# One written order for all engines, and a softplus that stays in its PSUM bank

## The chip, the cores and the metric

The kernel runs on one core of a Trainium2 chip. The metric is the device time of one execution in microseconds (us), lower is better. TensorE (PE) does the matmuls, VectorE (DVE), ScalarE (ACT) and GpSimd (POOL) work on the tiles between them, SyncE (SP) starts the DMAs. Each engine runs its own instructions strictly in the order in which the program gives them, and waits on semaphores for what other engines produce.

## The reference

Three layers, each fed by the one before, all in float32:

```
attention   4 batches x 8 heads, x [512, 64] and state [32, 64] per head:
            x reads the state by softmax, the state reads x by softmax; 544 rows per batch
MoE 1       h = x @ w_in ;  g = softplus(h) ;  y = g @ w_out        d_model 512, d_ff 2048
MoE 2       silu(y @ w_gate) * (y @ w_val) @ w_out                  d_model 512, d_ff 1536
```

## The kernel before

**Numbers.** A float32 matrix product is made of three products of shorter floats (`mm3`, L90): each operand is split into a high part, written by ScalarE, and a low part, whole minus high, written by `low` (L93). So every operand of a product costs a ScalarE pass and a VectorE or GpSimd pass, and each product is a high·high, a low·high and a high·low matmul.

**Stages.** The first 60 us or so are the attention. Then come the 64 units of MoE 1, numbered n = 0 to 63: d_ff is cut into four chunks c of 512, a chunk goes over the four batches b, and each of these over four pieces ft of 128 columns. A unit's first product `p1` (named pn here, 6 matmuls, L90 `ph`) puts h into one PSUM bank. ScalarE takes the softplus of it twice, once rounded into the high part `h` and once whole into a tile `C` in SBUF (class `Softplus`, L477 and L480). GpSimd makes the low part (`g_low`, gln here). The second product (Pn, `py`, 12 matmuls) runs several units later. From about 350 us on stand the 24 steps of MoE 2, named q, a, b, c, th and tL in the written order, with w_gate, w_val and w_out split piece by piece ahead of them.

**Seven products.** For three pairs of batches (chunk 1 batches 2 and 3, called pair 1 here; chunk 2 batches 2 and 3, pair 2; chunk 3 batches 0 and 1, pair 3) the second product is done as a 2 x 2 block product with seven instead of eight products. The blocks of g are B11 and B21 (first batch, ft 0-1 and 2-3) and B12 and B22 (second batch). `g_sum` (L598, VectorE) forms T1 = B12 − B11, T3 = B22 − B12, T2 = T3 + B11 and T4 = B21 − T2 for each of two halves f; T3 overwrites B12's SBUF tile. Each sum is split (`g_split_high` on ScalarE, L604; `g_split_low` on GpSimd). The products run in the order P1, P2, P5, P3, P6, P7, P4 (`y_part`, `pyPP`), 12 matmuls each, in units 24 to 30, 40 to 46 and 48 to 54. Each has two halves i in two banks. P6, P7 and P4 go on accumulating in P1's banks, P3 in those of P5. After each product `y_part_add` adds both halves to the running sum `yacc` (`y_put`, L533, VectorE; yan and ybn here for i = 0 and 1). P3 may write into P5's banks only after VectorE has read P5 out of them: P27 waits for ya26 and yb26, P43 for ya42 and yb42, P51 for ya50 and yb50.

**Weights.** Beside this the weights of the next chunk are loaded and split by `Piece`: ab ("size", ScalarE), hd ("head", L144, VectorE), tl ("tail", L155 and L158, two VectorE passes), wh (ScalarE) and wl (GpSimd). The piece's name follows: w is w_in, o is w_out of MoE 1, e are the pieces of MoE 2. In the traces they are `t_win`, `t_wo` and `t_gv`. `m_pair` folds w_in into the state's matmul (`pm`): mm on PE, mh on ScalarE, ml on VectorE (`m`, L93).

**PSUM.** There are eight banks of 128 x 512 floats. Tiles are requested by a tag ("y", "h" or "m"), and one that finds no free bank waits until an older one has been read.

**What sets the order.** Two passes with a manual schedule. The head (up to unit 8) is a written list, `ORDER`. From unit 9 on, a loop over n runs hooks (`at(n, kind, ...)`) of the kinds load, pe, dve0, act, pool, dve2, dve1, act1, pool1, so an operation's place is a rule, the same in each pair. MoE 2 has steps of its own (`at2`).

Of the kernel before, what the change touches and what calls it, by code (L numbers as in the profile page):

```python
# [18 lines left out]
LOADS = "x00 x01 st x21 x20 w0 x11 x10 x31 x30 w3 w2 n20 n21 w1 n01 n11 n10 n00 n31 o1 o0 o3 n30 o2"  # L19
ORDER = (  # L20
# [11 lines left out]
)  # L32

FIRST = 9


@with_exitstack
def attention_moe_moe2_kernel(
# [77 lines left out]
    class Piece:  # L116
# [52 lines left out]
        def low(self):  # L169
            low(nc.gpsimd, self.out[:, 1, :], self.t, self.out[:, 0, :])  # L170
# [14 lines left out]
    class GatePiece(Piece):  # L185
# [11 lines left out]
        def low(self):  # L197
            super().low()
# [16 lines left out]
        def split_sums(self):
            o = slot([P, 2, 512], F32R, self.place(), f"split_{self.name}")
            nc.scalar.activation(o[:, 0, :], self.s, AF.Copy)  # L217
            low(nc.gpsimd, o[:, 1, :], self.s, o[:, 0, :])
# [4 lines left out]
    class OutPiece(Piece):  # L223
# [8 lines left out]
        def low(self):  # L232
            super().low()
# [4 lines left out]
        def sums(self):  # L238
            pass

        def split_sums(self):
            pass
# [3 lines left out]
    def second_piece(f, part, late=False):  # L246
# [17 lines left out]
    class OutSums:  # L264
# [10 lines left out]
        def whole(self):  # L275
            self.t = []
            for f, r in enumerate(self.raw):
                t = rawp.tile([P, 512], F32, tag="tmade", bufs=3, name=f"w2t{self.q}_{f}")
                nc.vector.tensor_tensor(out=t, in0=r[:, 0].bitcast(F32), in1=r[:, 1].bitcast(F32), op=ALU.add)
                self.t.append(t)  # L280

        def sums(self):
            (a11, a21), (a12, a22) = ((t[:, :256], t[:, 256:]) for t in self.t)
            self.s = [rawp.tile([P, 512], F32, tag="sums", bufs=2, name=f"w2u{self.q}_{k}") for k in range(2)]
            s = [self.s[k // 2][:, k % 2 * 256:(k % 2 + 1) * 256] for k in range(4)]
            for o, x, y, op in (
# [3 lines left out]
                nc.gpsimd.tensor_tensor(out=o, in0=x, in1=y, op=op)  # L290

        def high(self):
            self.o = [slot([P, 2, 512], F32R, "made", f"w2o{self.q}_{k}") for k in range(2)]
            for k, o in enumerate(self.o):
                nc.scalar.activation(o[:, 0, :], self.s[k], AF.Copy)

        def low(self):
            w2s_d[self.q] = dram.tile([P, 2, 2, 512], F32, tag=f"w2s{self.q}", name=f"w2s{self.q}_d")
            for k, o in enumerate(self.o):
                low(nc.gpsimd, o[:, 1, :], self.s[k], o[:, 0, :])  # L300
                nc.sync.dma_start(out=w2s_d[self.q][:, k], in_=o.bitcast(F32))
# [15 lines left out]
    room = ["y"]  # L317

    class Item:
# [50 lines left out]
        def minus(self):  # L370
            m1 = self.mine("m1", 16)
            nc.gpsimd.tensor_tensor(
# [14 lines left out]
        def times(self):  # L387
            r1 = self.mine("r1", 16)
            nc.gpsimd.tensor_tensor(
# [11 lines left out]
        def low(self):  # L401
            low(nc.gpsimd, self.out[:, 1, :], self.t2, self.out[:, 0, :])

        def turn_e(self):
            self.ps = bank(room[0], f"pa{self.n}")
# [7 lines left out]
        def read(self):  # L413
            b, par = self.b, self.par
            self.ps = bank(room[0], f"pr{self.n}")
# [14 lines left out]
    def st_turn(b):  # L430
        srp[b] = bank(room[0], f"psr{b}")
# [24 lines left out]
    def m_pair(c, b):  # L456
        for par, tag in enumerate("mh"):
            m_mm(c, b, par, tag)

    def m_pair_high(c, b):  # L460
        for par in range(NPAR):
            m_high(c, b, par)

    def m_pair_low(c, b):
        for par in range(NPAR):
            m_low(c, b, par)


    class Softplus:


        def __init__(self, ps, g, h):
            self.ps, self.g, self.h = ps, g, h
# [5 lines left out]
        def whole(self):  # L479
            nc.scalar.activation(self.g, self.ps, AF.Softplus)  # L480
# [4 lines left out]
    def p1(u):  # L485
# [15 lines left out]
    def g_low(u):  # L501
        if sp[u].h is None:
            return
        l = work.tile([P, 512], F32R, tag="GL", bufs=BIG, name="l%d_%d_%d" % u)
        low(nc.gpsimd, l, sp[u].g, sp[u].h)
# [6 lines left out]
    def p2(u):  # L512
        c, b, ft = u
        if ft == 0:
            for dt in range(KT):
                yps[dt] = bank("y", f"py{c}_{b}_{dt}")
        t = gT.pop(u)
        for dt in range(KT):
            mm3(yps[dt], [wo[c, ft].out[:, i, dt * P:(dt + 1) * P] for i in range(2)], t, ft == 0, ft == FT - 1)

    def y_add(c, b, dt):
        y_put(b, dt, yps[dt], c == 0)
# [11 lines left out]

    SEVEN = {(1, 1), (2, 1), (3, 0)}
# [13 lines left out]
    class WoSums:  # L549
# [5 lines left out]
        def sums(self):  # L555
# [6 lines left out]
            for o, x, y, op in (  # L562
# [3 lines left out]
                nc.vector.tensor_tensor(out=o, in0=x, in1=y, op=op)  # L566

        def high(self):
            for k in range(2):
                o = ws[self.c, k, self.i] = slot([P, 2, 512], F32R, "ws", f"ws{self.c}_{k}_{self.i}")  # L570
                nc.scalar.activation(o[:, 0, :], self.s[k], AF.Copy)

        def low(self):
            for k in range(2):
                o = ws[self.c, k, self.i]
                low(nc.gpsimd, o[:, 1, :], self.s[k], o[:, 0, :])
# [11 lines left out]
    def g_sum(c, q, t, f):  # L588
# [4 lines left out]
        a, b = (g_whole(c, q, k, f) for k in (x, y))  # L593
        if at is None:
# [3 lines left out]
        nc.vector.tensor_tensor(out=o, in0=a, in1=b, op=op)  # L598
# [12 lines left out]
    def y_part(c, q, part):  # L611
        kind, k, t = OUTS[part]
        keep = KEEP[part]
        for i in range(2):
            if part in OPENS:
                ypx[keep, i] = bank("y", f"pyP{part}_{c}_{q}_{i}")
            ps = ypx[keep, i]
# [91 lines left out]
    def s4(c):  # L709
        if c == 0:  # L710
            ys[0] = const.tile([P, DM], F32, tag="yo", bufs=2, name="ys")
            nc.vector.tensor_copy(ys[0], tps["s3"])
        else:
            nc.vector.tensor_tensor(out=ys[0], in0=tps["s3"], in1=ys[0], op=ALU.add)

    def turn_ys():
        yT[0] = const.tile([P, 2, KT, P], F32R, tag="sy", name="yT")
        v = turn_mm(ys[0], KT, "ys")
        nc.scalar.activation(yT[0][:, 0], v, AF.Copy)
        low(nc.vector, yT[0][:, 1], v, yT[0][:, 0])  # L720
# [9 lines left out]
    banks = [0]  # L730

    def quad_bank(name):
        banks[0] += 1
        return bank("h" if banks[0] % 4 else "m", name)
# [13 lines left out]
    def split_act(key, src):  # L748
        h = work.tile([P, 512], F32R, tag="AH", bufs=7, name="h%d_%s" % key)
        l = work.tile([P, 512], F32R, tag="AL", bufs=7, name="l%d_%s" % key)  # L750
        nc.scalar.activation(h, src, AF.Copy)  # L751
        low(nc.gpsimd, l, src, h)
        act[key] = (h, l)

# [14 lines left out]

    def out_mm(n, j, dt):  # L770

        q = n % NF // 2
        b = 2 * (n // NF) + j
        ps = bank("y", f"po{n}_{j}_{dt}")
        for f in range(2):
            mm3(ps, [w2[n + f][:, i, dt * P:(dt + 1) * P] for i in range(2)], act[n + f, j], f == 0, f == 1)
        out_add(b, dt, ps, q == 0)
        if q == NQ - 1:
            out_store(b, dt)


# [3 lines left out]
    def out_part(n, part):  # L785
# [498 lines left out]
```

## Time and profile before

| | |
|---|---|
| median of 3 runs | 742.68 us (742.31 to 744.7) |
| the profiled execution | 743.8 us, its span 742.0 us |
| mean granted clock of TensorE over the span | 0.983 |
| DMA | 134.88 MB, mean 182 GB/s |

The span is the time from the first to the last instruction of the profiled execution; 1.8 us lie around it. Page section 2 cuts the span into 40 slices and gives the busy tenths of every engine in each; PE stands at 9 in nearly all, with exceptions that the tables by stretch show better. A busy PE there can also be one at half the clock: the granted clock stands beside it.

### The profile page before, as it was taken

How to read it: one execution, taken by the hardware profiler on the slowest of the kernel's cores; microseconds unless marked ns; L12 is line 12 of the kernel's file. 1: busy time of each engine (PE TensorE's matmuls, PEld its weight loads, DVE VectorE, ACT ScalarE, POOL GpSimd, SP SyncE). 2: the span in 40 equal slices, each digit the busy share in tenths (PEclk: the TensorE clock that was granted, in tenths of full speed). 3: DMA queues.
4: the chain of work that ended last, by engine and by line, in shares of the span. 5: the costliest groups of instructions: out<-in, count | busy, mean ns of one | idle time of the engine just before them, and what ended most of it. 6: DMA issues, size and time to landing. Idle time of an engine off the chain costs nothing.

```text
span 742.0 us, 10249 instructions
## 1 busy us (share of the span) xinstructions
PE 710.4 (96%) x3654; PEld 567.1 (76%) x3654; DVE 548.0 (74%) x768; ACT 345.5 (47%) x641; POOL 456.1 (61%) x355
## 2 busy tenths in 40 slices
PE   5699999999899979899999999999999999999997
PEld 1477877786678767688888888888888888888885
DVE  5875553789679897958489988889785666665564
ACT  3876464635454436443355544454453334343231
POOL 2467634698668786864157776577786367464252
PEclk9899999999899999999999999999999999999999
DMA  9910202253124330081463886767559997969303
GB/s 341 408 61 28 86 29 57 59 198 114 57 86 159 126 114 1 0 315 62 157 213 99 276 292 247 250 246 282 199 210 361 353 333 283 374 216 343 122 1 114
DMA packets 48627, 134.88 MB, mean 182 GB/s; under 512 B 5441, under 2 KB 17729, under 8 KB 48577
## 3 DMA queue, kind: packets, MB, share of 16 engines
q1 hardware_dynamic: 48576, 134.24, 50.9%
q8 instruction: 28, 0.46, 0.2%
q14 instruction: 23, 0.18, 0.1%
HBM read 93.06 MB, written 41.16 MB: 181 GB/s over the span
## 4 chain that ended last, share of the span: by engine, by line
PE 76%; DVE 15%; ACT 3%; issue 2%; POOL 2%; DMA 1%; SPq 0%; DVEq 0%; ACTq 0%
PE px L90 16%; PE py L90 16%; PE po L90 8%; PE ph L90 8%; PE pz L90 8%; PE poP L90 6%; PE pyPP L90 5%; PE pt L90 3%; DVE C L598 2%; PE ps L687 2%; DVE yacc L533 2%; PE pm L446 1%; PE ps L90 1%; DVE m L93 1%; DVE t_wo L155 1%
## 5 line engine op out<-in xcount | busy, mean ns | idle before, releaser
L93 POOL TENSOR_TENSOR l<-C,h 128x512 fp32r<-128x512 f32 x58 | 83.8, 1449 | 48.1 <-ACT C L480 42.7
L90 PE MATMUL ph<-aT,m 128*128 128x512 f32 x384 | 100.1, 399 | 0.2 <-DVE m L93 0.2
L90 PE MATMUL py<-h,wo 128*128 128x512 f32 x320 | 99.4, 391 | 0.9 <-POOL wo L93 0.8
L90 PEld LDWEIGHTS ph<-aT,m 128*128 128x128 f32 x384 | 71.3, 190 | 24.9 <-issue 7.5
L90 PEld LDWEIGHTS py<-h,wo 128*128 128x128 f32 x320 | 60.0, 188 | 14.5 <-POOL wo L93 1.6
L90 PE MATMUL po<-h,w 128*128 128x512 f32 x224 | 69.6, 392 | 0.0
L90 PE MATMUL py<-l,wo 128*128 128x512 f32 x160 | 62.3, 390 | 0.0
L93 POOL TENSOR_TENSOR split_gv<-sums_gv,split_gv 128x512 fp32r<-128x512 f32 x24 | 35.4, 1473 | 31.7 <-ACT split_gv L217 26.1
L477 ACT ACTIVATE h<-ph 128x512 fp32r<-128x512 f32 x58 | 34.4, 592 | 42.4 <-PE ph L90 42.3
L765 DVE TENSOR_TENSOR oacc<-poP,oacc 128x512 f32<-128x512 f32 x62 | 40.7, 687 | 10.3 <-PE poP L90 10.3
L90 PEld LDWEIGHTS po<-h,w 128*128 128x128 f32 x224 | 41.6, 188 | 8.5
L1139 POOL TENSOR_TENSOR cC<-cC,cB 128x512 f32<-128x512 f32 x24 | 32.0, 1332 | 21.0 <-ACT cB L1138 15.1
L90 PE MATMUL po<-l,w 128*128 128x512 f32 x112 | 43.7, 390 | 0.0
L480 ACT ACTIVATE C<-ph 128x512 f32<-128x512 f32 x64 | 38.0, 594 | 9.0 <-PE ph L90 9.0
L765 DVE TENSOR_TENSOR oacc<-po,oacc 128x512 f32<-128x512 f32 x48 | 31.9, 684 | 13.9 <-PE po L90 13.7
L93 POOL TENSOR_TENSOR l<-cA,h 128x512 fp32r<-128x512 f32 x14 | 19.9, 1418 | 32.8 <-ACT h L751 31.2
L90 PE MATMUL px<-T_0s,gw 128*128 128x512 f32 x135 | 38.1, 390 | 0.7 <-ACT cA L1177 0.7
L1203 DVE TENSOR_TENSOR cA<-py,cA 128x512 f32<-128x512 f32 x22 | 15.1, 685 | 31.8 <-PE py L90 26.6
L90 PE MATMUL px<-T_1s,gw 128*128 128x512 f32 x135 | 38.0, 389 | 0.0
L93 POOL TENSOR_TENSOR gv<-t_gv,gv 128x512 fp32r<-128x512 f32 x24 | 34.3, 1430 | 5.4 <-ACT gv L167 5.4
L533 DVE TENSOR_TENSOR yacc<-pyPP,yacc 128x512 f32<-128x512 f32 x42 | 28.4, 683 | 8.9 <-PE pyPP L90 8.9
L90 PEld LDWEIGHTS py<-l,wo 128*128 128x128 f32 x160 | 30.0, 188 | 6.3
(263 smaller groups left out, 1870.2 us busy)
## 6 DMA issues: line engine op xcount, KB each, us to landing
gw<-gv_d SPq DMA_DIRECT2D x60, 512.0 KB, 7.8
gv_d<-gv SPq DMA_DIRECT2D x24, 512.0 KB, 6.5
gv_d<-split_gv SPq DMA_DIRECT2D x24, 512.0 KB, 4.9
raw_win<-in_moe_w_in_dram SPq DMA_DIRECT2D x16, 512.0 KB, 6.5
raw_wo<-in_moe_w_out_dram SPq DMA_DIRECT2D x16, 512.0 KB, 3.6
w<-w_d SPq DMA_DIRECT2D x13, 512.0 KB, 9.4
raw_gv<-in_moe_w_gate_dram SPq DMA_DIRECT2D x48, 128.0 KB, 3.6
raw_gv<-in_moe_w_val_dram SPq DMA_DIRECT2D x48, 128.0 KB, 3.5
```

The source lines that it names most:

```text
L90: nc.tensor.matmul(o, a[s], b[t], start=first and i == 0, stop=last and i == 2, **k)
L93: eng.tensor_tensor(out=o, in0=whole, in1=high.bitcast(F32), op=ALU.subtract)
L155: nc.vector.scalar_tensor_tensor(out=ti, in0=self.top, scalar=-0x80000000, in1=ti, op0=ALU.bitwise_and, op1=ALU.bitwise_or,)
L446: nc.tensor.matmul(ps[k * NS:(k + 1) * NS, :], st[q, k, b, :], win[c, k].t[q, :], start=True, stop=True)
L477: nc.scalar.activation(self.h, self.ps, AF.Softplus)
L480: nc.scalar.activation(self.g, self.ps, AF.Softplus)
L533: nc.vector.tensor_tensor(out=v, in0=ps, in1=v, op=ALU.add)
L598: nc.vector.tensor_tensor(out=o, in0=a, in1=b, op=op)
L687: nc.tensor.matmul(gs[c][:, f], win[c, kt].t[:, f], sw[:, kt, :], start=kt == 0, stop=kt == KT - 1)
L765: nc.vector.tensor_tensor(out=v, in0=ps, in1=v, op=ALU.add)
L1139: nc.gpsimd.tensor_tensor(out=c["C"], in0=c["C"], in1=c["B"], op=ALU.mult)
L1203: nc.vector.tensor_tensor(out=c["A"], in0=y, in1=c["A"], op=ALU.add)
```

## The change

One table `ORDER` now names every operation of the whole program, 2121 names, and a loop runs it from front to end; the hooks, `at`, `at2` and the loops over n are gone. Functions that did several things are cut into one per operation, so that each has a name; many get their engine as an argument ("!" behind a name means the other one of VectorE and GpSimd). The operations themselves are the same, with the same engines, but for the softplus below. On SP, x11's load goes behind x31's, and one weight load (lw21) ahead of another piece's; on PE one group of six matmuls (s3m.4) moves some 10 us ahead.

The order changes on VectorE, ScalarE and GpSimd in a few dozen places, the most of them in the head and in the three pairs. For the first pair, VectorE's order before and after (/0 and /1 are the two passes of a tail):

```
before  hd.e1.0 tl.w22 tl.e1.0 ya23 yb23 yc23 yd23 g.T1110 hd.o20 ml.200 ml.201 g.T1111 ya24
        g.T3110 yb24 hd.o22 g.T2110 ya25 g.T3111 yb25 tl.o22 ml.210 ml.211 g.T2111 ya26 g.T4110
        yb26 tl.o20 g.T4111 ya27
after   hd.e1.0 tl.w22 tl.e1.0 ya23 yb23 yc23 yd23 g.T1110 hd.o20 ml.200 ml.201 g.T1111 ya24
        gl30 g.T3110 yb24 hd.o22 g.T2110 gl31 g.T3111 tl.o22 yb25 ml.210 ml.211 ya26 ya25 g.T4110
        yb26 g.T2111 tl.o20 g.T4111 ya27
```

For the second pair:

```
before  hd.w33 tl.w33 hd.e2.1 tl.w32 tl.e2.1 ya39 yb39 yc39 yd39 g.T1210 hd.o30 ml.300 ml.301
        g.T1211 ya40 g.T3210 yb40 hd.o32 g.T2210 ya41 g.T3211 yb41 tl.o32 ml.310 ml.311 g.T2211
        ya42 g.T4210 yb42 tl.o30 g.T4211 ya43
after   tl.w32 hd.w33 tl.w33 hd.e2.1 tl.e2.1 ya39 yb39 yc39 yd39 g.T1210 hd.o30 ml.300 ml.301
        g.T1211 ya40 gl46 g.T3210 hd.o32 yb40 g.T3211 g.T2210 ya41 gl47 yb41 ml.310 ya42 tl.o32
        g.T2211 g.T4210 yb42 tl.o30 ml.311 g.T4211 ya43
```

In the third pair gl54 and gl55 are put in behind ya48 and ya49; else the order around ya50 stays. On ScalarE, ab.e1.0 goes ahead of sh.e0.1. In the head, tl.o03 goes ahead of S5, S4 and r4 on VectorE, and wl.o03 ahead of ti5 on GpSimd. In MoE 2, a3.1 goes ahead of tl.e3.1.

The softplus of the second batch of each pair:

```diff
     class Softplus:
-        def __init__(self, ps, g, h):
+        def __init__(self, ps, g, h, stay=False):
...
         def whole(self):
-            nc.scalar.activation(self.g, self.ps, AF.Softplus)
+            if self.stay:
+                nc.scalar.activation(self.ps, self.ps, AF.Softplus)
+            if self.g is not None:
+                nc.scalar.activation(self.g, self.ps, AF.Copy if self.stay else AF.Softplus)
...
-        g = work.tile([P, 512], F32, tag="G", bufs=BIG, name=f"C{n}")
-        if (c, b // 2) in SEVEN and b % 2 and ft < 2:
-            sp[u] = Softplus(ps, g, None)
+        seven = (c, b // 2) in SEVEN and b % 2
+        g = None if seven and ft >= 2 else work.tile([P, 512], F32, tag="G", bufs=BIG, name=f"C{n}")
+        h = None if seven and ft < 2 else work.tile([P, 512], F32R, tag="GH", bufs=BIG, name=f"h{n}")
+        sp[u] = Softplus(ps, g, h, seven)
...
+    def g_low(u, eng):
         l = work.tile([P, 512], F32R, tag="GL", bufs=BIG, name="l%d_%d_%d" % u)
+        if sp[u].g is None:
+            low(nc.vector, l, sp[u].ps, sp[u].h)
         else:
-            sp[u] = Softplus(ps, g, work.tile([P, 512], F32R, tag="GH", bufs=BIG, name=f"h{n}"))
...
+            low(eng, l, sp[u].g, sp[u].h)
...
-    def g_sum(c, q, t, f):
+    def g_sum(c, q, t, f, eng):
...
         a, b = (g_whole(c, q, k, f) for k in (x, y))
+        if x in ("B12", "B22"):
+            a = sp[c, 2 * q + 1, BLOCK[x][1] + f].ps
```

So of the second batch, units ft 0 and 1 (block B12: units 28, 29, 44, 45, 52 and 53) get their softplus in place in the bank, and then a ScalarE copy of it to SBUF. Units ft 2 and 3 (B22: 30, 31, 46, 47, 54, 55) get the high part into SBUF and the softplus in place; they have no whole tile in SBUF any more. T1 and T3 read B12 and B22 from the bank, and the low part of the six B22 units is made by VectorE from the bank instead of by GpSimd from SBUF. A bank is then held until VectorE has read it for T1, or for T3 and the low part.

## Rows read from the trace of the kernel before

**Rows 1.** Stretches: PE, PEld, DVE, ACT, POOL busy us (instructions), granted clock, DMA share, GB/s.

```profile
180.00:200.00 20.00, 15.81 (x73) 12.89 (x72) 15.66 (x18) 6.99 (x14) 13.88 (x9) 0.83 0.25 79
260.00:280.00 20.00, 15.79 (x79) 12.97 (x78) 18.40 (x23) 7.97 (x16) 15.31 (x10) 0.91 0.32 105
300.00:320.00 20.00, 17.58 (x70) 13.68 (x69) 17.86 (x22) 10.21 (x20) 17.36 (x13) 0.91 0.13 37
```

**Rows 2.** Waits of PE: what for, us in total, times, longest.

```profile
PE pyPP L90 <- DVE yacc L533: 10.7, 3, 4.2
```

**Rows 3.** Timeline of PE at its gaps: start, us, instructions, [idle before <- releaser].

```profile
60.52 0.50 PE L90 MATMUL py<-h,wo 128*128 128x512 f32 x1 [0.84 <-POOL wo L93]
...
188.42 1.22 PE L90 MATMUL pyPP<-h,ws 128*128 128x512 f32 x2 [4.19 <-DVE yacc L533]
...
269.85 1.22 PE L90 MATMUL pyPP<-h,ws 128*128 128x512 f32 x2 [4.21 <-DVE yacc L533]
...
310.29 1.16 PE L90 MATMUL pyPP<-h,ws 128*128 128x512 f32 x2 [2.27 <-DVE yacc L533]
...
382.94 0.97 PE L90 MATMUL px<-T_0s,gw 128*128 128x512 f32 x3 [0.68 <-ACT cA L1177]
```

**Rows 4.** The chain that ended last, pieces in order of time: start, us, what.

```profile
57.03 1.44 DVE t_wo L158
...
188.42 5.49 PE pyPP L90 x12
...
199.14 2.74 PE pyPP L90 x12
...
269.85 4.41 PE pyPP L90 x12
...
310.29 4.62 PE pyPP L90 x12
```

**Rows 5.** Timeline of DVE before the first gap.

```profile
162.63 1.07 DVE L144 TENSOR_SCALAR t_gv<-t_gv 128x512 int32<-128x512 int32 x1 [2.40 <-ACT t_gv L135]
...
169.44 2.48 DVE L533 TENSOR_TENSOR yacc<-py,yacc 128x512 f32<-128x512 f32 x4
...
181.99 1.18 DVE L155 SCALAR_TENSOR_TENSOR t_wo<-raw_wo,t_wo 128x512 int32<-128x512 int32 x1
183.21 1.66 DVE L158 SCALAR_TENSOR_TENSOR t_wo<-raw_wo,t_wo 128x512 int32<-128x512 int32 x1
...
185.99 1.78 DVE L598 TENSOR_TENSOR C<-C,C 128x512 f32<-128x512 f32 x1
187.69 0.68 DVE L533 TENSOR_TENSOR yacc<-pyPP,yacc 128x512 f32<-128x512 f32 x1
```

**Rows 6.** Groups of instructions: busy us, mean ns of one | idle before.

```profile
L533 DVE TENSOR_TENSOR yacc<-pyPP,yacc 128x512 f32<-128x512 f32 x42 | 28.4, 683 | 8.9 <-PE pyPP L90 8.9
L598 DVE TENSOR_TENSOR C<-C,C 128x512 f32<-128x512 f32 x18 | 22.8, 1269 | 0.0
L93 POOL TENSOR_TENSOR l<-C,h 128x512 fp32r<-128x512 f32 x58 | 83.8, 1449 | 48.1 <-ACT C L480 42.7 <-PE pyPP L90 5.3
```

**Rows 7.** Timeline of ACT before the first pair.

```profile
161.42 0.63 ACT L217 ACTIVATE split_gv<-sums_gv 128x512 fp32r<-128x512 f32 x1 [2.23 <-POOL sums_gv L213]
161.96 0.64 ACT L135 ACTIVATE t_gv<-raw_gv 128x512 f32<-128x512 f32 x1
```

**Rows 8.** Timeline of DVE before the second and the third gap.

```profile
243.50 1.01 DVE L144 TENSOR_SCALAR t_gv<-t_gv 128x512 int32<-128x512 int32 x1 [2.48 <-ACT t_gv L135]
...
269.11 0.68 DVE L533 TENSOR_TENSOR yacc<-pyPP,yacc 128x512 f32<-128x512 f32 x1
...
309.56 0.68 DVE L533 TENSOR_TENSOR yacc<-pyPP,yacc 128x512 f32<-128x512 f32 x1
```

**Rows 9.** Timeline of PE: the first product of unit 30.

```profile
168.85 1.65 PE L90 MATMUL ph<-aT,m 128*128 128x512 f32 x6
```

**Rows 10.** Timeline of DVE in MoE 2: the first pass of tl.e3.1.

```profile
378.46 1.59 DVE L151 SCALAR_TENSOR_TENSOR t_gv<-t_gv,raw_gv 128x512 int32<-128x512 int32 x1
```

More of the change, by code (lines that the diff above doesn't have):

```diff
@@ L236, in low, with second_piece @@
             nc.sync.dma_start(out=w2_d[self.f], in_=self.out.bitcast(F32))
[L238 to L242, printed above, removed]
     made = {}
-    def second_piece(f, part, late=False):
+    EARLY = {(f, part) for f in range(3) for part in range(2)} | {(0, 2)}
+    def second_piece(f, part):
+        late = (f, part) not in EARLY
         return OutPiece(f, late) if part == 2 else GatePiece(f, part, late)
@@ L289, in sums, with high, low @@
             ):
[L290 to L301, printed above, removed]
+                eng.tensor_tensor(out=o, in0=x, in1=y, op=op)
+            self.o = {}
+        def high(self, k):
+            self.o[k] = slot([P, 2, 512], F32R, "made", f"w2o{self.q}_{k}")
+            nc.scalar.activation(self.o[k][:, 0, :], self.s[k], AF.Copy)
+        def low(self, k, eng):
+            if self.q not in w2s_d:
+                w2s_d[self.q] = dram.tile([P, 2, 2, 512], F32, tag=f"w2s{self.q}", name=f"w2s{self.q}_d")
+            o = self.o[k]
+            low(eng, o[:, 1, :], self.s[k], o[:, 0, :])
+            nc.sync.dma_start(out=w2s_d[self.q][:, k], in_=o.bitcast(F32))
     def load_w2s(q):
@@ L316, in attention_moe_moe2_kernel @@
     small = {}
-    room = ["y"]
     class Item:
@@ L456, in m_pair @@
     def m_pair(c, b):
-        for par, tag in enumerate("mh"):
+        for par, tag in enumerate("my" if c == 0 and b < 2 else "mh"):
             m_mm(c, b, par, tag)
[L460 to L466, printed above, removed]
     class Softplus:
-        def __init__(self, ps, g, h):
-            self.ps, self.g, self.h = ps, g, h
+        def __init__(self, ps, g, h, stay=False):
+            self.ps, self.g, self.h, self.stay = ps, g, h, stay
         def high(self):
@@ L729, in attention_moe_moe2_kernel, with quad_bank @@
     }
[L730 to L734, printed above, removed]
+    def quad_bank(n, k):
+        return bank("m" if (3 * n + k) % 4 == 3 else "h", f"p{'xzy'[k]}{n}")
     def quad_mm(ps, n, part, first):
@@ new lines, in attention_moe_moe2_kernel, with op, either @@
+        ops = {}
+        def op(name, fn, *args):
+            ops[name] = lambda: fn(*args)
+        def either(name, fn, *args, eng=nc.gpsimd):
+            other = nc.vector if eng is nc.gpsimd else nc.gpsimd
+            ops[name] = lambda: fn(*args, eng)
+            ops[name + "!"] = lambda: fn(*args, other)
+        for k in range(B * NPAR):
+            it = Item(*divmod(k, NPAR))
+            for key, step in (
+                ("sc", it.scores), ("mx", it.most), ("nm", it.negate), ("e", it.exp_tokens), ("rc", it.parts),
+                ("ts", it.turn_scores), ("M", it.maxima), ("ex", it.exps), ("S", it.sums),
+                ("r", it.parts_1), ("tu", it.turn), ("ah", it.high),
+                ("pa", it.turn_e), ("a", it.turned), ("pr", it.read), ("sr", it.mean),
+            ):
+                op(f"{key}{k}", step)
+            for key, step in (("mi", it.minus), ("ti", it.times), ("al", it.low)):
+                either(f"{key}{k}", step)
@@ L1010, in attention_moe_moe2_kernel @@
-        at(NU - 4, "pe", turn_ys)
-        for n in range(2):
-            at(NU - 5 + n, "load", load_gw, n)
-        at(NU - 3, "load", load_w2, 0)
+            op(f"ld.{name}", begin)
+            for tag, step in (("ab", "size"), ("hd", "head"), ("tl", "tail"), ("wh", "high"), ("sh", "split_high")):
+                op(f"{tag}.{name}", lambda step=step: getattr(store[key], step)())
+            for tag, step in (("wl", "low"), ("sm", "sums"), ("sl", "split_low")):
+                either(f"{tag}.{name}", lambda eng, step=step: getattr(store[key], step)(eng))
@@ new lines, in attention_moe_moe2_kernel, with softplus @@
+        for f in range(NF):
+            for part in range(3):
+                piece_ops(f"e{f}.{part}", made, (f, part), second_piece)
+        def softplus(u):
+            sp[u].high()
+            sp[u].whole()
+        for n, u in enumerate(units):
+            op(f"p{n}", p1, u)
+            op(f"sp{n}", softplus, u)
+            either(f"gl{n}", g_low, u, eng=nc.gpsimd)
+            c, q, k = u[0], u[1] // 2, n % (2 * FT)
+            if (c, q) in SEVEN:
+                part = SEQUENCE[k]
+                op(f"P{n}", y_part, c, q, part)
+                for i in range(2):
+                    op(f"y{'ab'[i]}{n}", y_part_add, c, q, part, i)
+            else:
+                op(f"P{n}", p2, u)
+                for dt in range(KT):
+                    op(f"y{'abcd'[dt]}{n}", y_add, c, u[1], dt)
@@ new lines, in attention_moe_moe2_kernel, with fresh, total, quad @@
+        op("tys", turn_ys)
+        op("tysh", turn_ys_high)
+        op("tysl", turn_ys_low)
+        NS2 = NPR * NF
+        cs = {n: {} for n in range(NS2)}
+        def fresh(n, k):
+            cs[n][k] = work.tile([P, 512], F32, tag=k, name=f"c{k}{n}")
+            return cs[n][k]
+        def total(eng, o, x, y, op):
+            eng.tensor_tensor(out=o(), in0=x(), in1=y(), op=op)
+        def quad(n, part):
+            if part in ("P1", "P5", "P2"):
+                k = ("P1", "P5", "P2").index(part)
+                cs[n]["xzy"[k]] = quad_bank(n, k)
+            quad_mm(cs[n][QUAD_KEEP[part]], n, part, part in ("P1", "P5", "P2"))
@@ L1246 @@
+                for name in names.split():
+                    ops[name]()
 _INS = ['moe_w_in', 'moe_w_out', 'moe2_w_gate', 'moe2_w_val', 'moe2_w_out']
```

635 lines of the change are left out of this document (203 added, 432 removed), and 141 rows, old and new, of tables (ORDER, STEPS).

## The prediction

> **What bounds the kernel now.** First the page: PE is busy 96% of the span, no other engine over 74%. So PE sets the time, and only PE's gaps, and the stretches in which it runs slowly, can be won back. The stretches show where these lie: three of 20 us have a granted clock below 1 and PE busy below 20 us [rows 1], and each holds one of the three pairs. The waits name the cause: three waits of a `pyPP` product for VectorE's `yacc`, 10.7 us in all [rows 2]. PE's timeline places them: P27 at 188.42 after 4.19 us, P43 at 269.85 after 4.21, P51 at 310.29 after 2.27 [rows 3]. The chain shows a second price. The twelve matmuls behind the wait take 5.49, 4.41 and 4.62 us, where the same twelve take 2.74 us at 199.14 [rows 4]: after the idle time the clock is at the lower of its two levels (1.2 against 2.4 GHz) for some of them, 0.83 on the mean of the first stretch [rows 1]. That is 2.75 + 1.67 + 1.88 = 6.3 us on top, 17.0 us together. Beside these there are a gap of 0.84 us in the head, for GpSimd's `wo`, and one of 0.68 us in MoE 2, for ScalarE's cA [rows 3]. All five are 18.5 us. That is the most that a better order could bring while the work stays, and PE's own work stays: the same matmuls in the same order but for one group.
>
> **Pair 1.** VectorE decides when P27 starts, so its queue is summed. Before, it idles 2.40 us ahead of hd.e1.0, for ScalarE's ab.e1.0 [rows 5]. This op stands on ScalarE behind sh.e0.1, which waits for GpSimd's sums while ScalarE idles 2.23 us [rows 7]. Moved ahead, ab.e1.0 fills that idle time, and hd.e1.0 starts at 160.2 instead of 162.63. Nothing else stands between it and ya23 in either order, so ya23 comes at 169.44 − 2.4 = 167.0 (what it reads, P23's first quarter, has been made by then). From ya23 to ya26 it is 187.69 − 169.44 = 18.25 us before [rows 5]. Of this:
> - ya25 (0.6 us from start to start, as the four adds in 2.48) and g.T2111 (1.7 to the next start) go behind ya26: −2.3.
> - gl30 and gl31 are new on VectorE: six such in all, two per pair, and no row shows this op. The nearest is `yacc`, one operand in PSUM and one in SBUF, 683 ns [rows 6], 0.6 us from start to start: +1.2. From above it is bounded by the slow two-SBUF-input op of 1.27 us, +2.5; below 0.6 nothing of this shape runs.
> - T3110 and T3111 read one operand from PSUM now. With both in SBUF an op of L598 takes 1269 ns on the mean, 1.78 at worst, beside a busy GpSimd; `yacc` takes 0.68 beside the same GpSimd, 42 times [rows 6]. I take 0.5 us off each: −1.0, bounds 0 and −2.2.
>
> ya26 so starts at 167.0 + 18.25 − 2.3 + 1.2 − 1.0 = 183.2 and ends at 183.9. P27 could start at 188.42 − 4.19 = 184.2. The wait goes, with 0.3 us to spare; yb26 ends three ops later, at 185.7, when the second half of P27 wants it (184.2 + 1.36). The gap with its slow matmuls is 4.2 + 2.75 = 6.9. As the margin is thin I leave 1.0 us of it standing: **−5.9**. GpSimd gives up two lows, which fills nothing on the path: its lows take 1.45 us each [rows 6] and its queue gets shorter. ScalarE has one op more per B12 unit, about 0.63 us each like its other passes [rows 7], and idles far more than that. tl.o22 (1.18 + 1.66 [rows 5]) now precedes yb25, whose bank p33 wants at 182.7; yb25 comes at about 182, still in time.
>
> The Trainium skill, "Perfetto Trace Analysis", section "Optimizing Scalar/DVE Operations", speaks against this part: a VectorE access to PSUM costs about 125 ns an instruction against 60 ns to SBUF. For twelve sums and six lows that would be an estimated 1.2 us more VectorE time in all. The row disagrees: `yacc`, with PSUM in it, is the faster one here, at 683 against 1269 ns [rows 6].
>
> **Pair 2.** VectorE idles 2.48 us ahead of hd.e2.1 [rows 8]. tl.w32 moves into that hole (2.8 us by the tail of [rows 5]), so ya39 and all behind it come some 2.4 us earlier. Ahead of ya42 no longer stand tl.o32 (2.8), g.T2211 (1.7) and ml.311 (0.6): −5.1; gl46 and gl47 do: +1.2; the two T3 are shorter: −1.0. ya42 moves from 269.11 to about 261.8, bound then by P42 itself, and P43, which could go at 269.85 − 4.21 = 265.6, starts on time. But yb42 stands behind the three ops that were put back: 262.5 + 2.8 + 1.7 + 0.6 + 0.7 gives 268.3 to 269.0, and P43's second half wants it at 267.0. I leave 2.0 us for that and 0.9 for P42, which needs banks and ya41 earlier than before, and for slow matmuls behind the rest: 4.2 + 1.7 − 2.9 = **−3.0**, bounds −5.9 and 0.
>
> **Pair 3.** ya50's place is not improved: hd.e0.2 and g.T2301 still precede it, gl54 and gl55 are added (+1.2), T3300, T3301 and T1301 get shorter (−1 to −2). With 2.27 + 1.88 = 4.15 at stake I take **−0.5**, from −4.1 to +1.
>
> **Head and MoE 2.** tl.o03 ends at 57.03 + 1.44 [rows 4]; ahead of it are now no longer S5, S4 and r4, and on GpSimd wl.o03 no longer follows ti5. Two us are more than the gap: **−0.9**. What is put back there (softmax of batch 2) is used some 20 us later. In MoE 2, a3.1 no longer waits behind tl.e3.1's pass of 1.59 us [rows 10], and 0.68 us with a little slow clock go: **−0.8**. s3m.4 and the two SP moves are worth nothing: PE has no gap where the group was or goes, and the loads are far from their uses; I bound them by ±0.3.
>
> **Sum.** −5.9 − 3.0 − 0.5 − 0.9 − 0.8 = −11.1 against the profiled execution's 743.8 (742.0 of span and 1.8 around it): 732.7. That execution is 1.1 above the median of 742.68, so on the median's scale **731.5**.
>
> **Rivals.**
> *All of it.* The change does what it can, all five gaps go: −18.5, 724.2. For it: VectorE is given time ahead of each pair, and less of it is spent beside GpSimd. Against: yb42 and ya50 by the sums above.
> *Half.* The margin of 0.3 us in pair 1 is an error in the other direction. If VectorE is 1.5 us late there, the clock falls again; half of pair 1's price stays (−3), half of pair 2's (−1.5), nothing of pair 3, head and MoE 2 as above (−1.7): −6.2, 736.5.
> *No difference.* The six lows are VectorE's, the engine that is late. If they take 1.27 us like two-input sums and T3 gets no shorter, each pair has 2.5 us more ahead of its wait, which takes up the 2.4 us won, and the waits stay: about 742.
> *Slower: PSUM runs out.* A bank of a second batch was free after ScalarE's pass; now it is held until VectorE has read it. At p30's start, 168.85 [rows 9], P23's four banks, the two of mm.20 and those of p28 and p29 are eight, so p30 needs ya23 first. It decides whether ya23 is done by 168.85. By the sum it is, at 167.7; at the old time, 170.1, p30 waits 1.3 us, p31's bank is read late too (gl31 and T3111, at about 182.6), P26, which opens two banks at 179.75, waits 2.9 and P27 still its 4. That is some 2.5 us more per pair, less the 1.7 of head and MoE 2 and what the shorter queue wins: about +5, 748. Against it: the 2.23 us of idle ScalarE are plain to see. The Trainium skill points this way too: "PSUM — Partial Sum Buffer", "Summary: rules for kernel authors", says to evacuate PSUM promptly; no run here shows yet what holding a bank costs.
>
> **How the numbers follow.** A difference under 0.3% (2.2 us) cannot be told from none. Forecast 0.50, all of it 0.17, half 0.18, no difference 0.05, slower 0.10. So faster 0.85, same 0.05, slower 0.10. The range from 724 to 740 takes in the first three with their own errors and leaves out the last two; the forecast's own is 727 to 735.
>
> **What would show it.** Right: hd.e1.0 near 160 without idle time ahead of it, ya26 ahead of ya25 and ending within half a us of p33's end, twelve matmuls of P27 in 2.7 to 3.2 us, the stretch from 180 to 200 with PE busy 19 or more; L93 with `ph` as an input on VectorE near 0.68 us, L598 with `ph` as well; a wait of 1 to 2 us inside P43. Wrong: PE waiting for VectorE at p30, P24 or P26 (a bank), T3 still at 1.2 us beside GpSimd, P51's gap gone in spite of hd.e0.2, or a new gap of PE outside the pairs.

## The result, and the profile after

The changed kernel takes 720.0 us (719.7 to 724.0, four runs), the one before 743.6 in the same set: a ratio of 0.9695, 95% interval 0.9656 to 0.9734. In a second set it took 720.3 against 743.4, 0.9684 (0.9671 to 0.9697). The forecast was 731.5, its range 724 to 740. The direction was right, the gain is twice what was forecast, and 720.0 is even under the 724.2 of "all of it".

PE runs the same 3,654 matmuls in nearly the same order in both traces, so the start of the same matmul in both tells where the time went:

```
PE starts at          before    after   difference   this stage   forecast
p1 (unit 1)            41.21    36.84      -4.4         -4.4         0
P4 (behind P3)         64.52    58.56      -6.0         -1.6        -0.9
mm.22 (behind pair 1) 201.82   188.68     -13.1         -7.2        -5.9
P50 (behind pair 2)   303.62   286.39     -17.2         -4.1        -3.0
p58 (behind P51)      314.75   293.19     -21.6         -4.3        -0.5
PE's last matmul ends 737.01   714.02     -23.0         -1.4        -0.8
end of the span        742.0    717.9     -24.1         -1.1         0
```

Two stages stand out: the first 41 us, where nothing was forecast, and pair 3. The 4.4 us of the first are at the upper end: the granted clock up to 40 us differs from run to run, and p1 starts at 36.8 to 39.9 us in the nine traces with the changed head that are used below, at 40.2 to 42.4 in the three with the old one, 2.8 us apart on the mean. The later stages agree within 0.1 us between two traces of the changed kernel.

The waits of PE for `yacc` [rows 2] are nearly gone. This is the row of the changed kernel (us in total, times, longest):

```profile
PE pyPP L202 <- DVE yacc L642: 1.0, 2, 0.5
```

P27, P43 and P51 stand without a gap ahead of them, and in the chain their twelve matmuls go at full clock, where they took 5.49, 4.41 and 4.62 us [rows 4]:

```profile
178.21 2.86 PE pyPP L202 x12
...
252.76 2.97 PE pyPP L202 x12
...
290.63 2.72 PE pyPP L202 x12
```

By stretches (columns as in [rows 1]), the changed kernel:

```profile
20.00:40.00 20.00, 16.32 (x347) 9.81 (x340) 19.90 (x42) 19.31 (x46) 10.71 (x10) 1.00 1.01 399
...
180.00:200.00 20.00, 20.00 (x116) 16.22 (x115) 13.21 (x20) 11.49 (x22) 14.71 (x11) 1.00 0.17 53
...
260.00:280.00 20.00, 19.03 (x100) 13.86 (x106) 18.97 (x28) 13.18 (x25) 14.59 (x11) 1.00 0.00 1
```

and the row of the kernel before that the prediction left out:

```profile
20.00:40.00 20.00, 15.05 (x285) 9.01 (x291) 18.04 (x36) 16.41 (x38) 8.20 (x8) 0.76 1.01 401
```

Here PE was busy 15 of 20 us at a granted clock of 0.76 before. This stretch was not weighed at all: the prediction took the head's only price from the one gap at 60.5. Now more matmuls go through it (347 against 285), at full clock in this profile and at 0.83 to 1.00 in the other eight.

VectorE ahead of P27 in the changed kernel:

```profile
154.22 0.68 DVE L256 TENSOR_SCALAR t_gv<-t_gv 128x512 int32<-128x512 int32 x1
...
159.94 2.73 DVE L642 TENSOR_TENSOR yacc<-py,yacc 128x512 f32<-128x512 f32 x4 [0.99 <-PE py L202]
...
164.76 1.02 DVE L256 TENSOR_SCALAR t_wo<-t_wo 128x512 int32<-128x512 int32 x1 [1.50 <-issue]
...
168.09 0.68 DVE L205 TENSOR_TENSOR l<-ph,h 128x512 fp32r<-128x512 f32 x1
168.69 0.68 DVE L708 TENSOR_TENSOR C<-ph,C 128x512 f32<-128x512 f32 x1
...
173.12 0.68 DVE L267 SCALAR_TENSOR_TENSOR t_wo<-raw_wo,t_wo 128x512 int32<-128x512 int32 x1
173.83 0.69 DVE L270 SCALAR_TENSOR_TENSOR t_wo<-raw_wo,t_wo 128x512 int32<-128x512 int32 x1
...
176.23 1.28 DVE L642 TENSOR_TENSOR yacc<-pyPP,yacc 128x512 f32<-128x512 f32 x2
```

hd.e1.0 starts without the 2.40 us of idle time [rows 5]. VectorE even waits for PE now, 0.99 us ahead of ya23. Ahead of hd.o20 it is idle for 1.50 us; the row names no releaser, but ScalarE's pass for the same piece, ab.o20, ends at 164.67:

```profile
164.01 0.66 ACT L247 ACTIVATE t_wo<-raw_wo 128x512 f32<-128x512 f32 x1
```

The new low and the sum with an operand in the bank take 0.68 us each. And the two passes of tl.o22, which nobody touched, take 0.68 and 0.69 us where they took 1.18 and 1.66. GpSimd stands idle beside the first and until 174.10, when the second has been running for 0.27 us:

```profile
174.10 1.58 POOL L205 TENSOR_TENSOR lT<-C,hT 128x512 fp32r<-128x512 f32 x1 [2.65 <-ACT hT L714]
```

ya26 ends at 176.9, 1.1 us ahead of P27's start at 178.04, instead of being the last to come.

### The profile page after: what moved, and what is told of

Its sections match the earlier page's. It is cut to its first block, busy times and chain, and to the rows that moved or that the text cites. A ratio compares the mean times of both kernels' runs of the same rounds, so it can differ in the third digit from the quotient of the medians.

```text
span 717.9 us, 10235 instructions
## 1 busy us (share of the span) xinstructions
PE 699.7 (97%) x3654; PEld 561.6 (78%) x3654; DVE 536.6 (75%) x774; ACT 349.3 (49%) x647; POOL 442.0 (62%) x349
## 4 chain that ended last, share of the span: by engine, by line
PE 94%; DVE 4%; DMA 1%; ACT 1%; issue 0%; SPq 0%; ACTq 0%
PE py L202 20%; PE px L202 18%; PE ph L202 12%; PE po L202 11%; PE pz L202 9%; PE pyPP L202 8%; PE poP L202 7%; PE pt L202 4%; PE pm L560 2%; PE ps L797 2%; PE ps L202 2%; DMA st<-in_st_dram 1%; DVE mx L459 1%; DVE t L479 1%; DVE m L482 0%; DVE yacc L642 0%
## 5 line engine op out<-in xcount | busy, mean ns | idle before, releaser
L205 POOL TENSOR_TENSOR l<-C,h 128x512 fp32r<-128x512 f32 x52 | 73.8, 1425 | 47.5 <-ACT C L589 45.4
L1090 DVE TENSOR_TENSOR cA<-py,cA 128x512 f32<-128x512 f32 x24 | 16.5, 686 | 39.9 <-PE py L202 26.1
L1107 ACT ACTIVATE cB<-px 128x512 f32<-128x512 f32 x24 | 14.4, 598 | 50.8 <-PE px L202 50.7
L589 ACT ACTIVATE C<-ph 128x512 f32<-128x512 f32 x58 | 34.7, 599 | 0.2
```

The costliest lines, as they stand in the source:

```text
L205: eng.tensor_tensor(out=o, in0=whole, in1=high.bitcast(F32), op=ALU.subtract)
L589: nc.scalar.activation(self.g, self.ps, AF.Copy if self.stay else AF.Softplus)
L1090: eng.tensor_tensor(out=o(), in0=x(), in1=y(), op=op)
L1107: op(f"{name}.{n}", lambda n=n, k=k: nc.scalar.activation(fresh(n, k), cs[n]["x"], AF.Copy))
```

## The experiments

The kernels were run in three sets of four, each timed against the kernel before in the same set (743.5, 743.3 and 743.4). The changed kernel's own nine runs are at 719.6 to 721.0 with one of 724.0. The head's clock moves a profile by up to 3 us, as said above, so small differences are read from the stages behind the head, by the start of the same matmul in both traces, and not from the medians.

**Order or softplus?** The first pair of kernels takes the change apart. *order_only* has the new table with the old softplus (against the changed kernel; `work.tile(...)` is cut short):

```diff
-        g = None if seven and ft >= 2 else work.tile(...)
+        stay = seven and (c, b // 2) in STAY
+        g = None if stay and ft >= 2 else work.tile(...)
...
-        sp[u] = Softplus(ps, g, h, seven)
+        sp[u] = Softplus(ps, g, h, stay)
...
+    STAY = set()
...
-        if x in ("B12", "B22"):
+        if x in ("B12", "B22") and (c, q) in STAY:
```

> The table as changed, but the softplus of the second batches goes to SBUF as before, and the six lows are GpSimd's again, at the table's places. By PE's instructions counted through, the change won 4.4 us in the head up to unit 1, 1.6 at P3, 7.2 in pair 1, 3.8 in pair 2, 4.7 in pair 3 and 1.4 in MoE 2. If the order does it: about 722 to 726, with P27 and P51 waiting under 1.5 us, and ya26 still on time. If the softplus in the bank does it (GpSimd has 9 us less to do, and VectorE's two-input operations run undisturbed): head, P3 and MoE 2 stay won, the three pairs do not, 733 to 737, with P27, P43 and P51 again waiting 2 to 4 us each.

*stay_only* has the new softplus, and its table gives every engine exactly the order of before:

> The order of before, name for name, with the softplus kept in the bank and the six lows on VectorE at the places where GpSimd's stood. If the order does it: 739 to 744, P27 and P43 still wait 3 to 4 us. If the softplus does it: 726 to 731, the three waits of pyPP under 1 us each, head and MoE 2 as before. If banks held longer run PSUM out: over 744, with PE waiting for VectorE at p30, P24 or P26.

order_only took 732.4 us (ratio 0.9849, 0.9832 to 0.9866), stay_only 732.1 (0.9851, 0.9834 to 0.9867). Each alone brings about half: 11.1 and 11.5 us, 22.6 together, against the 23.1 to 23.6 of both. So neither theory holds alone; both times lie just outside the ranges of their two theories. The waits of the three pairs in order_only, and then in stay_only:

```profile
PE pyPP L195 <- DVE yacc L636: 8.5, 6, 3.2
```

```profile
PE pyPP L195 <- DVE yacc L635: 3.1, 4, 1.3
```

Before they were 10.7 us [rows 2]. By the stages order_only wins 2.3, 1.6 and 1.5 us in the three pairs, stay_only 5.0, 4.2 and 1.8, the changed kernel 7.2, 4.1 and 4.3. So in the first two pairs the softplus does most; the order does the head, P3 and MoE 2. That is not how the prediction divided it. VectorE in order_only, at T2110 and T3111 (merged, x2) and tl.o22:

```profile
173.71 3.47 DVE L703 TENSOR_TENSOR C<-C,C 128x512 f32<-128x512 f32 x2
177.10 1.77 DVE L260 SCALAR_TENSOR_TENSOR t_wo<-raw_wo,t_wo 128x512 int32<-128x512 int32 x1
178.91 1.63 DVE L263 SCALAR_TENSOR_TENSOR t_wo<-raw_wo,t_wo 128x512 int32<-128x512 int32 x1
```

The same four operations take 6.9 us here and 3.8 in the changed kernel, in the same order.

**What of the softplus?** It does two things: T1 and T3 read one operand from PSUM, and GpSimd loses six lows. *t_bank* gives GpSimd its lows back (`g = work.tile(...)` for all units, so that B22 is copied to SBUF too); *low_dve* is order_only with only the six lows moved:

```diff
-            low(eng, l, sp[u].g, sp[u].h)
+            seven = (u[0], u[1] // 2) in SEVEN and u[1] % 2
+            low(nc.vector if seven else eng, l, sp[u].g, sp[u].h)
```

> The changed kernel, but the B22 units too get a ScalarE copy of their softplus to SBUF, and GpSimd makes their low parts from it, as before; T1 and T3 still read the bank. So GpSimd has its 9 us of lows back, and VectorE's sums have one operand in PSUM. In the runs so far the order alone gives 732.4 and all 720.0. If it is the sums' operand in the bank that pays (T3 from 1.2 to 1.8 us down to 0.68): 721 to 724, T2 and the tails at what they take in the changed kernel. If it is GpSimd's relief, which lets VectorE's other two-input operations (T2, tails) run at 0.68 to 0.84 instead of 1.2 to 1.8: 728 to 732.

> The counterpart: the changed order, the softplus to SBUF as before, T1 and T3 from SBUF, but the six lows of the B22 units on VectorE, from SBUF, at the table's places. GpSimd is relieved of 9 us, VectorE has two-input operations of SBUF only. If GpSimd's relief pays: 721 to 726, with T2110 and tl.o22 as short as in the changed kernel. If the operand in the bank pays: 730 to 736, since the six lows add 0.7 to 1.8 us each.

t_bank: 724.1 us (0.974, 0.9715 to 0.9764). low_dve: 733.5 (0.9872, 0.9855 to 0.9889), not better than order_only. The operand in the bank pays, GpSimd's relief alone does not: low_dve wins only 2.6 us in the three pairs, order_only 5.4, t_bank 13.6. On top of the operand in the bank the relief, with the lows read from the bank too, is worth the 2.0 us from t_bank to the changed kernel's 15.6. PE's wait in t_bank and in low_dve:

```profile
PE pyPP L202 <- DVE yacc L642: 3.1, 4, 1.5
```

```profile
PE pyPP L195 <- DVE yacc L637: 10.3, 6, 3.3
```

The groups say why. First low_dve (mean ns behind the busy time): all 18 sums are shorter than before (1037 against 1269 [rows 6]), but the six lows have two operands in SBUF and take 1072 ns.

```profile
L704 DVE TENSOR_TENSOR C<-C,C 128x512 f32<-128x512 f32 x18 | 18.5, 1037 | 0.0
L198 DVE TENSOR_TENSOR l<-C,h 128x512 fp32r<-128x512 f32 x6 | 6.4, 1072 | 0.0
```

Then the changed kernel:

```profile
L708 DVE TENSOR_TENSOR C<-C,C 128x512 f32<-128x512 f32 x12 | 13.9, 1162 | 0.0
L267 DVE SCALAR_TENSOR_TENSOR t_wo<-raw_wo,t_wo 128x512 int32<-128x512 int32 x14 | 13.0, 926 | 0.1
L205 DVE TENSOR_TENSOR l<-ph,h 128x512 fp32r<-128x512 f32 x6 | 4.1, 676 | 0.0
L708 DVE TENSOR_TENSOR C<-ph,C 128x512 f32<-128x512 f32 x6 | 4.1, 676 | 0.0
```

and the tails' first pass in the kernel before:

```profile
L155 DVE SCALAR_TENSOR_TENSOR t_wo<-raw_wo,t_wo 128x512 int32<-128x512 int32 x14 | 16.3, 1164 | 0.1
```

In the changed kernel's trace 281 sums and lows of 128x512 on VectorE have one operand in PSUM: they take 0.66 to 0.69 us, the 134 of them beside a GpSimd that is busy all through as well as the 92 beside an idle one. The 113 sums and tail passes that read SBUF twice take 0.65 to 0.69 us beside an idle GpSimd (31) and up to 1.80 beside a busy one. The Trainium skill, "SBUF — State Buffer", section "Who interferes with whom", states this rule: a VectorE instruction with two SBUF inputs contends with a GpSimd instruction that reads SBUF; one with at most one does not, unless it runs in one of the modes that use two ports. These rows agree with it.

One thing more stands in these traces, and it gives the rule a price. The long operations do not run slower, they wait for the GpSimd operation that is running when they start. In the traces of before and after, 138 operations of VectorE with two SBUF operands of 128x512 take over 0.72 us: each started while a GpSimd operation was running, and each ended 0.545 to 0.555 us behind that operation's end. (Five more started within 0.1 us of the start or end of one and did not wait.) The heads (hd), with one SBUF operand, do the same, 0.28 us behind it: 0.41 us beside an idle GpSimd, up to 1.56 beside a busy one. So one SBUF operand alone does not spare an operation the wait.

```profile
169.89 0.41 DVE L256 TENSOR_SCALAR t_wo<-t_wo 128x512 int32<-128x512 int32 x1
...
261.94 1.52 DVE L256 TENSOR_SCALAR t_wo<-t_wo 128x512 int32<-128x512 int32 x1
```

**The moves that the prediction priced.** *no_fill* puts `ab.e1.0` back behind `sh.e0.1` and `tl.w32` back behind `hd.e2.1`. *ya_late* puts back what the order took from ahead of ya26 (ya25, g.T2111) and ya42 (tl.o32, ml.311, g.T2211). Both are otherwise the changed kernel.

> The changed kernel, with ab.e1.0 back behind sh.e0.1 and tl.w32 back behind hd.e2.1: the two moves that by the prediction win 2.4 us each for VectorE ahead of pairs 1 and 2. If these 2.4 us go into the waits as the prediction summed them, with 0.3 us to spare and slow matmuls behind: 725 to 728. If the changed kernel has slack there (VectorE idles 1.0 us ahead of ya23, 1.5 ahead of hd.o20 and 1.4 ahead of hd.o30 in it): 720.5 to 723.5, and what is lost shows as p30 and p46 waiting for a bank that ya23 and ya39 free.

> The changed kernel, with what the order put behind ya26 and ya42 put ahead of them again: ya25 and g.T2111 ahead of ya26, and tl.o32, ml.311 and g.T2211 ahead of ya42. By the prediction these are worth 2.3 us in pair 1 and 5.1 in pair 2. If they decide: P27 waits about 1 to 2 us and P43 3 us with slow matmuls behind, 724 to 728. If VectorE, with its shorter operations, is early enough (ya26 has 1.1 us to spare, ya42 1.8): P27 waits under 0.5 and P43 1 us, 720.5 to 722.5.

no_fill: 723.0 us (0.9727, 0.9706 to 0.9747). By the stages 1.4 us are lost, all at one place, where p30 waits for the bank that ya23 frees (0.3 of it is made good by mm.22); pair 2 loses nothing:

```profile
PE ph L195 <- DVE yacc L635: 1.3, 1, 1.3
```

So in the changed kernel VectorE has slack there, and the 2.4 us that carried the prediction's sums were not needed for P27. ya_late: 723.7 us (0.9734, 0.9716 to 0.9752), between the two expectations. By the stages 0.5 us come back in pair 1 and 1.7 in pair 2, 0.5 of it made good at P46:

```profile
PE pyPP L195 <- DVE yacc L635: 1.8, 2, 1.3
```

With the short operations of the changed kernel around them, these moves are worth 0 to 1.7 us each, where the prediction's sums had 2.4 for either of the first two, and 2.3 and 5.1 for what went behind ya26 and ya42.

**The head.** In the kernel before, ScalarE's sr1 idles for VectorE's rc2. First the kernel before, then the changed one:

```profile
29.80 0.31 ACT L428 ACTIVATE sr<-pr,rc 128x64 f32<-128x64 f32 x1 [2.78 <-DVE rc L359]
```

```profile
27.02 0.35 ACT L542 ACTIVATE sr<-pr,rc 128x64 f32<-128x64 f32 x1
```

sr1 reads batch 0's rc, which is long done; rc2 makes batch 1's. The program's addresses explain it: in the kernel before, sr of batch 0 (512 bytes a partition at 228480) overlaps batch 1's softmax sums sm (8 bytes at 228480), and rc2 is the last to read those. In the changed program nothing else lies on sr's tile. *sm_one* takes the overlap away in the kernel before:

```diff
-                small[name, self.b] = stat.tile([P, 2, n], F32, tag=name, name=f"{name}{self.b}")
+                if name == "sm":
+                    sm = stat.tile([P, B, 2, n], F32, tag=name, name="sm")
+                    for b in range(B):
+                        small[name, b] = sm[:, b]
+                else:
+                    small[name, self.b] = stat.tile([P, 2, n], F32, tag=name, name=f"{name}{self.b}")
```

> The kernel before, and only this: the softmax sums sm of the four batches lie in one tile instead of four. In the program of before, ScalarE's sr1 waits for VectorE's rc2, of which it reads nothing: sr's tile lies on the address of batch 1's sm, and rc2 is the last to read that. If this hidden wait costs the head its time: sr1 starts at 27.1 instead of 29.8, p0 some 2 us earlier and at full clock, 739.5 to 741.5. If VectorE's own order does it (ml.001 behind rc6 and r2, as here): less than 1 us, 742.5 to 744.

739.6 us (0.9953, 0.9938 to 0.9968), 2.4 to 4.6 us less, from one tile. sr1 now waits 0.46 us, for PE:

```profile
27.63 0.31 ACT L433 ACTIVATE sr<-pr,rc 128x64 f32<-128x64 f32 x1 [0.46 <-PE pr L424]
```

*head_old* is the changed kernel with the old order on all engines up to P8; *head_dve* only puts rc6 back behind S3 and ml.001 behind r2 on VectorE. *after_again* is the changed kernel, run with them.

> The changed kernel itself, once more, for the other kernels of this call: 719.5 to 724, the upper part where the matmuls around 36 us run at half the clock in the head. Both theories of the other runs are read against this one.

> The order of before up to unit 8's second product on all engines, then the changed one, softplus in the bank as changed. If the head is worth what PE's instructions counted through show, 4.4 us to unit 1 and 1.6 at P3: 4 to 6.5 us over the changed kernel of the same call, sr1 again waits for rc2 to 29.8, p0's matmuls at half the clock. If the 4.4 us are only the one profile's clock (other runs of the same head show 1.3 to 4.1): 1.5 to 3 us over it.

> The changed kernel with two operations of VectorE in the head back where they were: rc6 behind S3 and ml.001 behind r2, so that p0's second half waits for 1.9 us more of VectorE's queue; sr1 does not wait for rc2 here. If VectorE's queue ahead of ml.001 makes the head's gain: 2 to 4 us over the changed kernel of the same call. If the hidden wait of sr1 makes it: under 1.3 us over it.

after_again 720.3 us, head_old 725.9 (0.9756, 0.9741 to 0.9771), head_dve 721.0 (0.9699, 0.9685 to 0.9712). The head is worth 5.6 us with P3. Of VectorE's queue ahead of ml.001 0.7 us are seen, no more than the runs of either kernel scatter. In head_old the wait is back:

```profile
30.70 0.31 ACT L535 ACTIVATE sr<-pr,rc 128x64 f32<-128x64 f32 x1 [2.77 <-DVE rc L466]
```

By sm_one the hidden wait is 2.4 to 4.6 of the head's 5.6 us, probably most of them; sm_one's trace is of its slowest run and has p1 only 1.2 us earlier. No run puts this wait alone back into the changed kernel, and the other moves of the head were not taken apart.

**A version that is faster still?** *better* and *better2* go after the waits that are left in the changed kernel.

> The changed kernel, with the three waits of PE for VectorE that it still has in and behind pair 2 taken on: ya41 ahead of g.T3211 (P42 waits 0.4 us for it), ya44 and yb44 ahead of ml.320 (P45 waits 0.6), yb45 ahead of tl.o33 (P46 waits 0.7). If each wait is only the place in VectorE's queue: 1.5 to 1.7 us less, 718.3 to 718.7 against 720.0. If VectorE is simply behind there and the wait moves on to the next sum: 719.5 to 720.5.

> The three moves of better, and two more for the waits that these brought up: yb42 right behind g.T2211 and ahead of tl.o32 (P43's second half waited 1.2 us for it), hd.e0.2 behind yb50 (P51 waited 0.2 and 0.8 for ya50 and yb50). If the waits of pairs 2 and 3 are now only places in VectorE's queue: 1.5 to 2.5 us under the changed kernel of the same call, no wait of PE for yacc over 0.3 us. If VectorE has simply no time left there, and each us of PE gained is waited for at the next sum: within 0.7 us of it.

better: 721.9 us (0.9716, 0.9694 to 0.9738). By the stages 1.0 us is won in pair 2, and 1.2 come back in P51. better2: 723.3 (0.9726, 0.971 to 0.9741), 3.0 over the changed kernel of the same set, 2.7 of it in the stages behind the head. Neither beats the changed kernel, and both lie above the ranges of both their theories. better2 has one wait left, which is longer than all of the changed kernel's together:

```profile
PE pyPP L195 <- DVE yacc L635: 2.3, 1, 2.3
```

That is P45, for ya44. What stands ahead of it on VectorE are ws.30's four sums (0.91, 1.41, 1.51, 1.50 us here; 0.90, 1.40, 0.41, 0.41 in the changed kernel) and hd.o33. Two of the four now start while a GpSimd operation runs, by moves that never touched them; in the changed kernel they fall into 0.60 us in which GpSimd is idle.

## Why the prediction was wrong

The span got 24.1 us shorter, 13.0 more than the 11.1 of the forecast's sum. By stage, 5.1 of these 13.0 are the head, 3.8 pair 3, 1.3 pair 1, 1.1 pair 2, 0.6 MoE 2 and 1.1 what lies behind the last matmul. Two steps failed: the list of gaps that left out the head, and the price of VectorE's queue, which changed only the operations that the diff touches and kept every other at its old length.

**"The most that a better order could bring": wrong.** The prediction reads "three of 20 us" with a clock below 1 and PE busy below 20 us; by the same table there are five, 20 to 40 us (15.05 us busy at 0.76) and 40 to 60 (19.62 at 0.98) too. So the list of five gaps [rows 1 to 3] left out the head's worst stretch. The step "head −0.9" priced one gap of 0.84 and missed 5.1 us of 6.0 in these two traces, 4.7 of 5.6 by head_old's median. The wait behind it was to be read in the trace (2.78 us of idle ScalarE, for an operation whose output sr1 does not read); that the change would remove it was not to be read in the diff, since it hangs on SBUF addresses.

**Pair 1, −5.9: right in its place and its wait, −7.2 measured, but in part by luck.** On the old scale (6.0 added) hd.e1.0 starts at 160.2 without idle time, ya26 ends at 182.9 and P27 starts at 184.0; the forecast had 160.2, 183.9 and 184.2. The 1.0 us that was left standing did not stand. From ya23 to ya26 it is 16.29 us, the forecast's sum gives 16.15. The moves, the lows (0.6 each) and T3 (0.5 shorter each) came as summed. Two terms that the sum does not have cancel: tl.o22 is 1.5 us shorter, and 1.5 us pass idle ahead of hd.o20. And ya23 comes 1.1 us earlier than summed, since the four tail passes ahead of it take 4.13 us instead of 5.90.

"GpSimd gives up two lows, which fills nothing on the path" is the step that failed here. With the lows (+1.2) and T3 (−1.0) netted to nearly zero, the sum gives the softplus no share. But stay_only, without any new order, takes 6.4 us out of P27's part, after 1.35 added ahead of it by p30's wait for a bank. Its queue from ya23 to ya26 takes 15.65 us instead of 18.25 with nothing moved: T2110 and T2111 take 0.68 us each where they took 1.77 and 1.78 (the second in [rows 5]). No GpSimd operation holds them up: when they start, GpSimd is idle (178.34 to 181.92) or its operation is just ending (at 185.07).

```profile
178.55 0.68 DVE L701 TENSOR_TENSOR C<-C,C 128x512 f32<-128x512 f32 x1
...
185.04 0.68 DVE L701 TENSOR_TENSOR C<-C,C 128x512 f32<-128x512 f32 x1
```

**Pair 2, −3.0: −4.1 measured.** The wait for yb42 that was put at 2.0 us is not there: yb42 ends at 254.0, when P43's second half wants it, since tl.o32 took 1.5 us and not 2.8, and g.T2211 0.68 and not 1.7. The sum for yb42 also has ml.311 ahead of it, which the order puts behind, and leaves out g.T4210, which stands ahead; at 0.6 us each this changes nothing. A small wait for P42 (0.2) came, of the 0.9 that the forecast left there, and others behind it, at P45 and P46 (0.4 and 0.5).

**Pair 3, −0.5: the mis-sized term; −4.3 measured.** ya50's place is as it was, as said. But the operations ahead of it are not. Before, VectorE from ws.31's second sum to T1301, and GpSimd beside it:

```profile
294.70 1.40 DVE L566 TENSOR_TENSOR wsum<-wsum,t_wo 128x256 f32<-128x256 f32 x1
296.03 1.51 DVE L566 TENSOR_TENSOR wsum<-t_wo 128x256 f32<-128x256 f32 x1
297.46 1.50 DVE L566 TENSOR_TENSOR wsum<-t_wo,wsum 128x256 f32<-128x256 f32 x1
298.88 1.78 DVE L598 TENSOR_TENSOR T_1g<-C,C 128x512 f32<-128x512 f32 x1
...
295.78 1.47 POOL L93 TENSOR_TENSOR lT<-T_0g,hT 128x512 fp32r<-128x512 f32 x1
297.21 1.47 POOL L93 TENSOR_TENSOR l<-C,h 128x512 fp32r<-128x512 f32 x1
```

and after, where GpSimd is idle for 1.59 us beside the three sums:

```profile
276.35 0.43 DVE L676 TENSOR_TENSOR wsum<-wsum,t_wo 128x256 f32<-128x256 f32 x1
276.69 0.42 DVE L676 TENSOR_TENSOR wsum<-t_wo 128x256 f32<-128x256 f32 x1
277.02 0.42 DVE L676 TENSOR_TENSOR wsum<-t_wo,wsum 128x256 f32<-128x256 f32 x1
277.36 0.68 DVE L708 TENSOR_TENSOR T_1g<-ph,C 128x512 f32<-128x512 f32 x1
...
277.62 1.30 POOL L205 TENSOR_TENSOR wo<-t_wo,wo 128x512 fp32r<-128x512 f32 x1 [1.59 <-ACT wo L279]
```

4.2 us in four operations, of which the forecast had only T1301's part of the "−1 to −2" for three sums. order_only gets 1.5 us of this stage, stay_only 1.8, t_bank all: the sums need the bank and the order here, and why the order is needed, when ya50's place is the same, was not taken apart.

**MoE 2, −0.8: −1.4.** a3.1's gap went as said (−1.0). The other 0.4 came where s3m.4 was moved away, which was counted at nothing, within its bound of 0.3 but for a tenth. The span's last 1.1 us lie behind the last matmul: 5.0 us in the one profile of before, 4.3 in sm_one's, 3.8 to 3.9 in every other trace, stay_only's with the old order among them. So they are not shown to be the change's.

**The rivals.** "PSUM runs out" did not happen, but its place was right: no_fill and stay_only show p30 waiting 1.3 us for the bank of ya23, the length that was predicted. What it put behind this did not come: in stay_only P27 waits 0.49 us, not 4. By the trace of the changed kernel the order has ya23 early enough. "All of it" was the nearest, and it too rested on the short list. (The forecast's own sum, 742.68 − 11.1, gives 731.6; 731.5 is a slip of 0.1.)

## What to carry to other kernels

Price every stretch in which the granted clock or the busy time of the bounding engine is below full, before calling a sum of gaps the ceiling. Where VectorE is late and GpSimd works beside it, find the VectorE operations that are longer than their like, and look which GpSimd operation runs when they start: giving twelve sums one operand in PSUM was worth 8 us here (order_only against t_bank), moving the lows from one engine to the other nothing (low_dve). A wait for an operation whose output the waiting one does not read can be a shared address, as here, and one tile placed otherwise can remove it.

## What the runs showed of the hardware that was not expected

An operation of VectorE that reads SBUF twice, and a head pass, waits for the GpSimd operation that runs when it starts, and ends a fixed time behind that one's end (0.55 us for two operands of 128x512, 0.28 for a head). So the same 128x256 sum took 0.42 and 1.51 us, the same 128x512 pass 0.68 and 1.78. A move anywhere ahead shifts which operation meets which: better2's moves, which were to shorten VectorE's queue ahead of waits, cost 2.7 us behind the head, and better's 1.0 us won in pair 2 went again in pair 3. The 281 operations with an operand in PSUM did not wait.
